# A ConvNeXt-V2 block on one core: the layer-norm chain one slot shorter, and the first expansions two slots later

## The chip, the cores and the metric

The kernel runs on one NeuronCore of a Trainium2 chip. Five engines work side by side, each through its own instruction stream in order: PE (TensorE, matrix products into the eight PSUM banks), ACT (ScalarE), DVE (VectorE), POOL (GpSimd) and SP, which here only issues DMA transfers. The metric is device microseconds (us) from launch to end. Three timed runs of the kernel before took 1468.47, 1468.29 and 1466.35 us; the median is 1468.29 us.

## The reference

One image of 512 x 512 pixels with 96 channels in bfloat16. `K` is 3 and `E` is 384 hidden channels.

```python
for i in range(K):
    for j in range(K):
        out = out + xp[:, i:i+H, j:j+W, :] * dw[i, j][None, None, None, :]
h = _layernorm(out, axis=-1)
h = jnp.einsum('bhwc,ce->bhwe', h, w1)
h = _gelu(h)
gx = jnp.sqrt((h * h).sum(axis=(1, 2), keepdims=True) + 1e-6)
nx = gx / (gx.mean(axis=-1, keepdims=True) + 1e-6)
h = grn_gamma * (h * nx) + grn_beta + h
h = jnp.einsum('bhwe,ec->bhwc', h, w2)
return x + h
```

The sum of `h * h` runs over the whole image, so no output can be made before every pixel has been expanded and passed through the GELU once. The kernel therefore has two phases with a short global step between them.

## The kernel before, in words

The image is cut into 128 blocks of four image rows (`NBLK`, `GR`). Phase 1 is a software pipeline written as a list of numbered slots (the loop at line 852). In slot s the 3x3 convolution of block s runs, for s up to 127, and, once the pipeline is full, the expansion of an older block, called "mlp" in the code: its product with `w1` and the GELU. The distance between the two is the lag. A slot is thus one of three kinds: convolution alone (the ramp), convolution and expansion, or expansion alone (the tail, `NTAIL` slots, `mlp_tail`).

What happens to block b on the way:

- The convolution is three bursts of 24 matmuls (`conv_taps`) into three PSUM banks, `Y3`, banks 4 to 6. In some slots without an expansion, called spare, it takes the banks 0 to 3 that expansions would use. ACT copies the result out (`evac`, tile `y_bf`).
- The squares of `y_bf` are made by ACT in a slot without an expansion (`sqa`), else by POOL one slot later (`sqp`). PE adds up values and squares per pixel (`stage_stats`) into a part of PSUM bank 7.
- Blocks come in batches of 4 (the first three batches, blocks 0 to 3, are smaller and take a shorter path on DVE). When the last block of a batch has its sums, DVE makes the variances (`stage_var`, tile `var`) and clears the sums. POOL makes the first guess of 1/sqrt (`stage_rstd`: 2 small instructions) and two Newton steps (`stage_newton`: 8). DVE transposes the result (`stage_turn`, tile `rt`), SP writes it to DRAM (`stage_rows`, 2 transfers) and reads it back spread over partitions (`stage_bcast`, 4 transfers, tile `rbc`).
- POOL multiplies each block by its `rbc` (`stage_norm`, tile `yn`), SP writes it to DRAM (`stage_write`, 4 transfers) and, one slot later, reads it back in the layout of the expansion (`stage_read`, tile `ynT`).
- The expansion (`mlp_units`) is 9 GELU instructions on ACT of one or two banks each in a slot with a convolution, and 4 of three banks in the tail. DVE takes statistics of the GELU's output (`bst`); part of it is summed through PE instead (`gram_next`, also in bank 7). Every third block up to 111 is kept in DRAM as it is ("whole", 3 stores), the last even blocks stay in SBUF ("held"), and the others are expanded a second time in phase 2.

The slot of every step is set by the loop at line 820, through `put(slot, what, value)`. With `last_s` the slot of the batch's last sums, the old table is: moments at `last_s`, first guess at +1, Newton and turn at +2, rows at +3, bcast at +4, first multiplication at +5. Each later block of a batch follows one slot on; write, read and expansion come 1, 2 and 4 slots after the multiplication. The expansion of a batch whose first block is b0 so begins in slot b0 + 14.

Within one slot the order on each engine is fixed by the loop's text; every instruction keeps program order. SP: load of x for block s + 4, read, write, bcast, rows, one store of a whole block. POOL: Newton, square, multiplication, first guess. DVE in a slot with an expansion: two statistics, the transposes of x for block s + 3 (`turn_x`), two and two more statistics, the transpose of `rt`, the variances, the remaining statistics.

The slots worked out from that table: before, the slots without an expansion are 0 to 4, 7, 10 to 16 and 29, with expansions of blocks 0 to 3 in slots 5, 6, 8 and 9 and of block 4 in slot 17. Slot 29 is one because blocks 12 to 15 were squared by ACT, so their sums came a slot earlier, while block 16's batch took the longer way: block 16 is expanded two slots after block 15. From slot 30 to 127 every slot has both, and 128 to 141 are the tail.

Of the kernel before, what the change touches and what calls it, by code (L numbers as in the profile page):

```python
# [17 lines left out]
BATCH = 4  # L18
NHELD = 5
EVERY = 3  # L20
NTAIL = 14
GRB = 3


# [32 lines left out]
def kernel(  # L57
# [23 lines left out]
    NBLK = H // GR  # L81
# [7 lines left out]

    TAIL0 = NBLK - NTAIL  # L90
    HELD = [NBLK - 2 - 2 * i for i in range(NHELD)][::-1]
# [3 lines left out]
        return q in HELD  # L95

    def is_whole(q):
        return q < TAIL0 and q % EVERY == 0

    def cm_quads(q):  # L100
        if is_whole(q) or is_held(q):
            return NQ
        if q > HELD[0]:
            return 1
        return 2 if q >= NBLK - 16 or q % EVERY == 1 else 3

    whole = [q for q in range(NBLK) if is_whole(q)]
    g_dram = dram.tile([len(whole), 128, NQ * NCH * QW], bf16, name="g_dram")

# [51 lines left out]
    W2s = consts.tile([128, NCH, C], bf16, name="W2s")  # L161
    B2c = consts.tile([128, C], f32, name="B2c")
    free = [[q for q in range(NBLK) if is_whole(q)], list(HELD)]
    free = [v for i, q in enumerate(free[0]) for v in (free[1][i:i + 1] + [q])]
    made_q = KEPT + [q for q in range(NBLK) if not is_whole(q) and not is_held(q) and q not in KEPT]
# [17 lines left out]
    with ExitStack() as p1:  # L183
        pe, dve, act, pool, sp = (InOrder(tc, e) for e in (nc.tensor, nc.vector, nc.scalar, nc.gpsimd, nc.sync))
# [259 lines left out]
        def turn_x(b):  # L444
            xin = xins.pop(b)
            t = xt_ring[b % NXT]
            pairs = t[:, 0:2, :].rearrange("p i s -> p (i s)").bitcast(f32)
            dve.transpose(out=pairs.rearrange("p (g m) -> p g m", m=MB),
                          in_=xin[:, :, 0:64].bitcast(f32))
            dve.transpose(out=t[:, 2, :].rearrange("p (g m) -> p g m", m=MB), in_=xin[:, :, 64:96])  # L450
# [103 lines left out]
        def stage_rstd(k, eng):  # L554
            N = BATCHES[k][1] * GR * NG
            var = msts.pop(k)
            eng.tensor_scalar(out=var[:, :N], in0=var[:, :N], scalar1=3.0e38, scalar2=C * LN_EPS,
                              op0=ALU.min, op1=ALU.max)
            ri = small.tile([128, NS], i32, name="ri")
            eng.tensor_scalar(out=ri[:, :N], in0=var[:, :N].bitcast(i32), scalar1=-0.5, scalar2=float(0x5F3759DF),  # L560
                               op0=ALU.mult, op1=ALU.add)
            rcur = ri[:, :N].bitcast(f32)
            rns[k] = (var, rcur)

        def stage_newton(k, eng):
            N = BATCHES[k][1] * GR * NG
            var, rcur = rns[k]
            for it in range(NEWTON_ITERS):
                last = it == NEWTON_ITERS - 1
                t_ = small.tile([128, NS], f32, name="nt")  # L570
                eng.tensor_tensor(out=t_[:, :N], in0=rcur, in1=rcur, op=ALU.mult)
                eng.tensor_tensor(out=t_[:, :N], in0=t_[:, :N], in1=var[:, :N], op=ALU.mult)
                f = C ** 0.5 if last else 1.0
                eng.tensor_scalar(out=t_[:, :N], in0=t_[:, :N], scalar1=-0.5 * f, scalar2=1.5 * f,
                                  op0=ALU.mult, op1=ALU.add)
                rn = small.tile([128, NS], bf16 if last else f32, name="rstd" if last else "rn")
                if last and N % 32:
                    eng.memset(rn[:, N:(N + 31) // 32 * 32], 0.0)
                eng.tensor_tensor(out=rn[:, :N], in0=t_[:, :N], in1=rcur, op=ALU.mult)
                rcur = rn[:, :N]  # L580
            rns[k] = rn
# [72 lines left out]
        def stage_norm(b, eng=None):  # L654
            k = batch_of[b]
            b0, n = BATCHES[k]
            yn = ynpool.tile([128, NI, W], bf16, name="yn")
            (eng or pool).tensor_tensor(out=yn[:], in0=ybf.pop(b)[:],
                               in1=rbcs[k][:, b - b0:b - b0 + 1, :].to_broadcast([128, NI, W]), op=ALU.mult)
            yns[b] = yn  # L660
# [106 lines left out]
        def store_next():  # L767
            if stores:
                b, h = stores.pop(0)
                n = NCH * QW * NQ // 3  # L770
                sp.dma_start(out=g_dram[whole.index(b)][:, h * n:h * n + n],
                             in_=flat(b)[:, h * n:h * n + n])
# [41 lines left out]
        def put(s, what, v):  # L814
            at.setdefault((s, what), []).append(v)

        RAMP = 4
        last_norm = -1
        mlp_slots = set()
        for k, (b0, n) in enumerate(BATCHES):  # L820
            for b in range(b0, b0 + n):
                quick = b not in mlp_slots
                put(b if quick else b + 1, "sqa" if quick else "sqp", b)
                last_s = b + 1 if quick else b + 2
                put(last_s, "stats", b)
            ramp = b0 + n <= RAMP
            if ramp:
                put(last_s, "chain", k)
                put(last_s + 1, "spread", k)
            else:  # L830
                put(last_s, "moments", k)
                put(last_s + 1, "rstd", k)
                put(last_s + 2, "newton", k)
                put(last_s + 2, "turn", k)
                put(last_s + 3, "rows", k)
                put(last_s + 4, "bcast", k)
            for b in range(b0, b0 + n):
                last_norm = s = max(last_norm + 1, last_s + (1 if ramp else 5))
                put(s, "norma" if ramp else "norm", b)
                put(s + 1, "write", b)  # L840
                put(s + 2, "read", b)
                m = s + (3 if ramp else 4)
                mlp_slots.add(m)
                put(m, "mlp", b)
                put(m + is_whole(b), "combine", b)
                last_slot = m
# [2 lines left out]
        turn_x(0)  # L849
        turn_x(1)  # L850
        turn_x(2)
        for s in range(last_slot + 1):
            get = lambda kind: at.get((s, kind), [])
            if s + 4 < NBLK:
# [8 lines left out]
                stage_rows(k)  # L863
            store_next()
            for k in get("newton"):
                stage_newton(k, pool)
            for b in get("sqp"):
                stage_sq(b, False)
            for b in get("norm"):
                stage_norm(b)  # L870
            for k in get("rstd"):
                stage_rstd(k, pool)
            mlp = get("mlp")

            def spread_out():
# [2 lines left out]
                for b in get("norma"):  # L878
                    stage_norm(b, dve if b < 2 else pool)

            spare = not mlp and s % 2 == 1
            taps, evac = conv_taps(s, spare) if s < NBLK else ([], None)
            if mlp and mlp[0] >= TAIL0:
                assert not taps
# [26 lines left out]
            else:  # L911
                b = mlp[0]
# [165 lines left out]
```

## Time and profile before

| what | value |
|---|---|
| median of three timed runs | 1468.29 us |
| the profiled execution, its time | 1471.49 us |
| the profiled execution, its span | 1469.7 us |
| PE, ACT, DVE, POOL busy in the span | 95%, 95%, 80%, 87% |
| slots 0 to 16, first copy of a convolution to the first GELU of block 4 | 12.19 to 97.28 us |
| slots of both kinds, copy of block 30 to copy of block 127 | 198.06 to 880.25 us, 97 slots of 7.03 us |
| GELU of the tail, one slot | about 5.35 us |
| mean granted TensorE clock | 0.994 |

All durations below come from the one profiled execution. Its time is 3.2 us over the median of the timed runs and 1.8 us over its own span. In the timeline a row gives the start, the time from the first to the last of a merged run of equal instructions, the engine, the operation with its tiles, how many there were, and in brackets how long the engine sat idle before and what released it. In a table of stretches each column gives the busy time of one engine in that stretch, then the granted clock of TensorE (PEclk), the share of the DMA engines' time and the bytes moved.

### The profile page before, as it was taken

The numbers are of one execution on the slowest core, as the hardware profiler recorded it, in microseconds if no ns is written. First come the engines' busy times: TensorE is split into PE (matmuls) and PEld (weight loads), VectorE is DVE, ScalarE is ACT, GpSimd is POOL, SyncE is SP. The second block draws the span as 40 slices with busy tenths as digits, with TensorE's granted clock in tenths as the row PEclk, the third lists the DMA queues.
The fourth block names the chain that finished last, engine by engine and source line by source line (L and its number), as shares of the span: only waits on it lengthen the run. The fifth ranks groups of instructions, "written<-read, shape, count | busy, mean of one in ns | idle before, by whom it ended". The sixth has DMA issues, their size and how long they took to land. (4 is left out here: it accounts for less than half of the span.)

```text
span 1469.7 us, 54337 instructions
## 1 busy us (share of the span) xinstructions
PE 1391.7 (95%) x23105; PEld 816.2 (56%) x23105; DVE 1171.2 (80%) x2232; ACT 1401.4 (95%) x1583; POOL 1278.9 (87%) x864
## 2 busy tenths in 40 slices
PE   7889989999999999999999998789999999999998
PEld 3344444444444444444444455467777777767776
DVE  7749989999999999999999996865555555545555
ACT  6889979999999999999999999999999999989997
POOL 2549899999999999999999896569999999999998
PEclk9999999999999999999999999999999999999999
DMA  5577889889888988888988876659999999999998
GB/s 169 177 216 221 258 259 287 269 261 280 266 261 277 285 249 268 280 271 272 278 265 264 267 244 174 194 194 398 331 356 396 412 396 394 409 387 389 405 399 333
DMA packets 169210, 430.30 MB, mean 293 GB/s; under 512 B 34374, under 2 KB 84230, under 8 KB 164102
## 3 DMA queue, kind: packets, MB, share of 16 engines
q1 hardware_dynamic: 152292, 318.52, 66.5%
q0 software_dynamic: 15312, 108.14, 19.2%
q8 instruction: 181, 2.97, 0.8%
q14 instruction: 63, 0.52, 0.1%
q10 hardware_dynamic: 1362, 0.15, 0.1%
HBM read 265.70 MB, written 160.94 MB: 290 GB/s over the span
## 5 line engine op out<-in xcount | busy, mean ns | idle before, releaser
L35 ACT ACTIVATE g<-PS 128x512 bf16<-128x512 f32 (+2 forms) x1062 | 735.5, 938 | 10.4 <-PE PS L35 9.3
L35 DVE BATCH_NORM_STATS2 bst<-g 128x6 f32<-128x512 bf16 x1107 | 669.9, 673 | 35.7 <-ACT g L35 35.6
L35 ACT ACTIVATE gr<-PS 128x1536 bf16<-128x1536 f32 x348 | 485.9, 1456 | 26.6 <-PE PS L35 21.5
L35 DVE TENSOR_TENSOR o_sb<-PS,xb 128x384 bf16<-128x384 f32 x512 | 275.9, 557 | 223.2 <-PE PS L35 148.7
L35 POOL TENSOR_TENSOR yn<-y_bf,rbc 128x1536 bf16<-128x1536 bf16 x126 | 391.3, 3108 | 55.2 <-DMA rbc<-r_dram 34.6
L324 POOL TENSOR_TENSOR xb<-xr,B2c 128x1536 f32<-128x1536 bf16 x118 | 368.0, 3133 | 1.4
L35 PE MATMUL PS<-xT,Wq 64*32 64x511 bf16 (+1 forms) x9198 | 341.2, 389 | 27.0 <-ACT y_bf L35 11.0
L35 PE MATMUL PS<-ynT,w1p 128*128 128x512 bf16 x1158 | 340.0, 380 | 17.1 <-ACT g L35 5.3
L35 POOL TENSOR_TENSOR ysq<-y_bf 128x1536 bf16<-128x1536 bf16 x114 | 313.2, 2748 | 38.4 <-ACT y_bf L35 35.8
L35 PE MATMUL PS<-ynT,w1s 128*128 128x512 bf16 x984 | 266.8, 380 | 0.0
L35 PEld LDWEIGHTS <-gr 128*128 128x128 bf16 x4152 | 203.7, 98 | 54.7 <-ACT gr L35 0.7
L35 ACT ACTIVATE y_bf<-PS 128x1536 bf16<-128x1536 f32 (+2 forms) x135 | 207.7, 1544 | 16.7 <-PE PS L35 12.6
L35 PEld LDWEIGHTS <-Wq 64*32 64x32 bf16 x9216 | 112.9, 90 | 198.7 <-PE PS L35 112.0
L35 PE MATMUL PS<-W2s,gr 128*128 128x96 bf16 x4080 | 213.1, 206 | 0.3 <-DVE o_sb L35 0.2
L35 DVE STREAM_TRANSPOSE xT<-xin 128x576 f32<-128x576 f32 (+1 forms) x256 | 181.4, 749 | 13.8 <-DMA xin<-in_x_dram 13.7
L35 PEld LDWEIGHTS <-w1p 128*128 128x128 bf16 x1158 | 97.0, 97 | 168.9 <-issue 123.0
L35 PEld LDWEIGHTS <-g 128*128 128x128 bf16 x1716 | 105.8, 98 | 89.1 <-issue 56.0
L35 PE MATMUL PS<-w1p,ynT 128*128 128x256 bf16 (+2 forms) x828 | 125.2, 272 | 7.3 <-ACT xT L35 2.8
L35 PE MATMUL PS<-g 128*128 128x128 bf16 x1476 | 123.8, 220 | 5.9 <-DVE PS L35 5.9
L35 PEld LDWEIGHTS <-gl 128*128 128x128 bf16 x1824 | 90.5, 98 | 41.0 <-issue 20.1
L35 PE MATMUL PS<-W2s,gl 128*128 128x96 bf16 x1824 | 98.1, 207 | 13.1 <-DVE o_sb L35 13.0
L35 PEld LDWEIGHTS <-w1s 128*128 128x128 bf16 x984 | 78.4, 98 | 39.0 <-issue 0.6
(110 smaller groups left out, 672.9 us busy)
## 6 DMA issues: line engine op xcount, KB each, us to landing
g_dram<-g SPq DMA_DIRECT2D x114, 512.0 KB
gl<-g_dram POOLq DMA_DIRECT2D x38, 1536.0 KB, 10.8
xin<-in_x_dram SPq DMA_DIRECT2D x126, 432.0 KB
yn_dram<-yn SPq DMA_DIRECT2D x512, 96.0 KB
ynT<-yn_dram SPq DMA_DIRECT2D x128, 384.0 KB
out_dram<-o_sb SPq DMA_DIRECT2D x127, 384.0 KB
xr<-in_x_dram POOLq DMA_DIRECT2D x123, 384.0 KB, 6.7
ynT<-yn_dram SPq DMA_DIRECT2D x246, 128.0 KB
```

The lines of the kernel that those rows point to most:

```text
L35: r = f(*a, **k)
L324: pq.tensor_tensor(out=xb[:], in0=grp[q]["xr"][:], in1=bias[:, None, :].to_broadcast([128, PXP, C]), op=ALU.add)
```

## The change

Four things, in one edit:

- `stage_rstd` moves from the end of POOL's part of slot `last_s + 1` to right before `stage_newton`, and both now stand at the start of slot `last_s + 1`, ahead of POOL's square and multiplication. Turn, rows, bcast and the first multiplication each move one slot forward. The lag becomes 13, and `NTAIL` 13.
- Blocks 0 to 3 are expanded in slots 7 to 10 instead of 5, 6, 8 and 9.
- A slot without an expansion is spare when it is the second, fourth and so on of a run of such slots, instead of when its number is odd.
- The set of whole blocks keeps its old bound, written as a number.

```diff
-NTAIL = 14
+NTAIL = 13
...
     def is_whole(q):
-        return q < TAIL0 and q % EVERY == 0
+        return q < NBLK - 14 and q % EVERY == 0
...
+        FIRST_MLP = 7
...
-                put(last_s + 1, "rstd", k)
-                put(last_s + 2, "newton", k)
-                put(last_s + 2, "turn", k)
-                put(last_s + 3, "rows", k)
-                put(last_s + 4, "bcast", k)
+                put(last_s + 1, "newton", k)
+                put(last_s + 1, "turn", k)
+                put(last_s + 2, "rows", k)
+                put(last_s + 3, "bcast", k)
             for b in range(b0, b0 + n):
-                last_norm = s = max(last_norm + 1, last_s + (1 if ramp else 5))
+                last_norm = s = max(last_norm + 1, last_s + (1 if ramp else 4))
...
-                m = s + (3 if ramp else 4)
+                m = b + FIRST_MLP if ramp else s + 4
...
+        alone = 0
...
             for k in get("newton"):
+                stage_rstd(k, pool)
                 stage_newton(k, pool)
             for b in get("sqp"):
                 stage_sq(b, False)
             for b in get("norm"):
                 stage_norm(b)
-            for k in get("rstd"):
-                stage_rstd(k, pool)
...
-            spare = not mlp and s % 2 == 1
+            alone = 0 if mlp else alone + 1
+            spare = alone > 0 and alone % 2 == 0
```

Worked out from the new table: the slots without an expansion are 0 to 6 and 11 to 16; the expansions of blocks 0 to 3 stand in slots 7 to 10, that of block 4 still in slot 17, and from there every slot up to 127 has both. Slot 29 now has the expansion of block 16. The tail is slots 128 to 140. Spare are 1, 3, 5, 12, 14 and 16 (before: 1, 3, 7, 11, 13, 15 and 29). Block 114 is expanded beside the last convolution instead of in the tail. The arithmetic and the amount of data moved are the same.

## The prediction, made before the changed kernel ran

> **What bounds the kernel now.** I read the page first, then a table of stretches cut where the slots change kind, then ACT's timeline in the stretches with idle time, then the rows of one batch on POOL and DVE. The page's first part:
>
> ```profile
> PE 1391.7 (95%) x23105; PEld 816.2 (56%) x23105; DVE 1171.2 (80%) x2232; ACT 1401.4 (95%) x1583; POOL 1278.9 (87%) x864
> ```
>
> Two engines at 95% don't say where time can be won. The stretches do (PE, weight loads, DVE, ACT and POOL busy, then clock and DMA):
>
> ```profile
> 180.39:198.06 17.67, 13.26 (x224) 5.88 (x223) 14.19 (x28) 10.27 (x15) 15.48 (x6) 0.81 0.78 231
> 198.06:880.25 682.19, 664.22 (x11933) 331.14 (x11931) 669.33 (x1240) 682.16 (x972) 630.81 (x446) 1.00 0.87 269
> 880.25:961.87 81.62, 65.74 (x635) 42.86 (x633) 64.95 (x128) 78.99 (x62) 50.19 (x28) 1.00 0.61 184
> ```
>
> In the 97 full slots ACT is busy 682.16 of 682.19 us: ACT is the bound, at 682.19 / 97 = 7.03 us a slot. PE stands at 97%, DVE at 98%, POOL at 92%, so all three have little to give. The tail is ACT's too (78.99 of 81.62). Work on ACT is the same after the change but for one square, so the change wins only where ACT is idle. That is ahead of 97 us, in the ramp, and in the first stretch shown: 7.4 us of its 17.67. ACT there, slots 28 to 30:
>
> ```profile
> 180.39 1.51 ACT L35 ACTIVATE y_bf<-PS 128x1536 bf16<-128x1536 f32 x1
> 181.72 2.08 ACT L35 ACTIVATE g<-PS 128x1024 bf16<-128x1024 f32 x3
> 185.81 1.51 ACT L35 ACTIVATE y_bf<-PS 128x1024 bf16<-128x1024 f32 x2 [2.02 <-PE PS L35]
> 187.42 1.48 ACT L35 ACTIVATE ysq<-y_bf 128x1536 bf16<-128x1536 bf16 x1
> 193.36 1.51 ACT L35 ACTIVATE g<-PS 128x1024 bf16<-128x1024 f32 x2 [4.46 <-PE PS L35]
> 195.71 2.49 ACT L35 ACTIVATE g<-PS 128x512 bf16<-128x512 f32 x4 [0.84 <-PE PS L35]
> 198.06 1.49 ACT L35 ACTIVATE y_bf<-PS 128x1536 bf16<-128x1536 f32 x1
> ```
>
> Copies of blocks 28, 29 and 30. Slot 29 has no expansion, and ACT waits for PE three times. PE's rows say why:
>
> ```profile
> 189.50 1.44 PE L35 MATMUL PS<-g 128*128 128x128 bf16 x12 [3.14 <-DVE PS L35]
> 190.87 1.48 PE L35 MATMUL PS<-xT,Wq 64*32 64x512 bf16 x24
> ```
>
> PE stood 3.14 us until DVE had cleared the sums in bank 7, as `gram_next` follows the variances at once in such a slot, and then ran slowly: 24 matmuls of a convolution took 1.48 us, against 0.87 in full slots.
>
> **Part 1: slot 29 becomes a full slot, and one tail slot goes.** Copy 28 to copy 30 is two slots in 17.67 us. After, every slot from 17 to 127 is full. Between copy 28 and copy 127 there are 17.67 + 97 x 7.03 before and 99 x 7.03 after, so 2 x 7.03 - 17.67 = -3.61 us. The tail loses one slot:
>
> ```profile
> 917.01 5.66 ACT L35 ACTIVATE g<-PS 128x1536 bf16<-128x1536 f32 x4
> 922.33 5.71 ACT L35 ACTIVATE xT<-PS 128x1536 bf16<-128x1536 f32 x4
> ```
>
> 922.33 - 917.01 gives 5.3, and 5.35 over the next ones. Sum: -3.61 - 5.35 = **-8.96**. Checked by work: it is the 7.3 us of ACT's idle time, the square of 1.48, and small change. That square goes to POOL, 2.75 us, where 8% are free.
>
> **Part 2: the ramp.** From slot 0 to slot 10 both orders hold 11 convolutions, 7 squares on ACT and 4 expansions. Before, ACT ends them at 74.06, after waits of 2.71 (for the first `ynT`), 1.00, 0.19, 3.31 (slot 7: spare convolution waits for the expansions' banks) and 1.08 us from slot 5 on, 8.3 in all. After, slots 5 and 6 are two more convolutions, during which the first `ynT` lands, and slots 7 to 10 are full ones without a change of banks. I leave 1.1 us of wait for slot 5 (slot 4 had 1.11) and 0.6 for slot 7 (the convolution's first burst waited 0.64 to 0.90 for its banks): slot 10 ends at 74.06 - 8.3 + 1.7 = 67.5. The next six slots, 11 to 16, end when block 4 can be expanded. That hangs on a chain. Variances of blocks 4 to 7: end of slot 9, at 67.5 - 7.0 - 0.4 = 60.1. `rt` on DVE 6.55 later (below): 66.7. From `rt` to the first multiplication took 72.48 to 83.44, POOL waiting 12.49 us for `rbc` before it: 10.96, so 77.6. Newton steps for blocks 8 to 11 now stand ahead of it on POOL: their variances came 1.4 after copy 12 (78.52 to 79.9), copy 12 is due at 72.3 by steps of 3.4 to 4.0 a slot, and 3.6 us of Newton end at 77.3, hidden behind `rbc`. From that multiplication to the first GELU of block 4 took 97.28 - 83.44 = 13.84: 91.4, against 97.28, so -5.9. Bounds: convolution alone (3.43 a slot, copies at 71.10 and 74.53) would give 88.7, so -8.6; a chain that is no earlier gives 0.
>
> In that chain PE waits some 2 us for `ynT` in slot 17. Rows: after 3.14 us idle it ran slowly, as shown, and after an idle 1.88 us at 46.7 a convolution of 72 took 4.13 us, against 2.81. So I add 1.5 us, 0.62 for three matmuls of the first unit (1.44 against 0.82) and 0.84 for the wait at 195.71: **-4.4**. [...]
>
> **Part 3: the chain in every batch, 28 times in full slots.** One batch before, on DVE and on POOL:
>
> ```profile
> 419.15 0.22 DVE L35 TENSOR_TENSOR var<-PS,neg 128x64 f32<-128x64 f32 x1
> ...
> 432.95 0.23 DVE L35 STREAM_TRANSPOSE rt<-rstd 128x64 bf16<-128x64 bf16 x1
> ```
>
> ```profile
> 423.61 0.24 POOL L35 TENSOR_SCALAR var<-var 128x64 f32<-128x64 f32 x1
> ...
> 448.56 3.11 POOL L35 TENSOR_TENSOR yn<-y_bf,rbc 128x1536 bf16<-128x1536 bf16 x1
> ...
> 674.58 3.11 POOL L35 TENSOR_TENSOR yn<-y_bf,rbc 128x1536 bf16<-128x1536 bf16 x1 [0.78 <-DMA rbc<-r_dram]
> ```
>
> The 10 small POOL instructions take 3.55 us (423.61 to 427.14) wherever they stand. New wait one: POOL's first guess waits for `var`, and square and multiplication queue behind it. Without waits POOL needs 3.55 + 4 x 5.78 (a square and a multiplication, 427.14 to 432.91) = 26.7 us a batch, the batch has 4 x 7.03 = 28.1, so it may idle 1.4. It now does so here instead of at squares (22.4 us of such waits from 200 to 870). Cost nothing. New wait two: `rt` waits for POOL, and DVE's statistics queue behind. `rt` stood 13.58 after the end of `var` (419.37); one slot less leaves 6.55, and 3.65 are needed: 2.9 us to spare. Cost nothing as long as POOL is less than that late. SP: two `rows` (1.19 us) and four `bcast` (2.55) move one slot forward, past a load of x, a read, four writes and a store; their order among themselves stays. The write after the first multiplication starts later, at `var` + 9.4 instead of + 7.5 (426.84), and holds SP that long; the expansion it feeds comes three slots on. The loop that can bind: POOL's first guess, multiplication, write, the read that waits for its landing, next write, `bcast`, `rbc`, multiplication, next first guess. It is the same before and after. Where POOL did not wait for `rbc`, its first guess to that multiplication took 24.95 (423.61 to 448.56), a ceiling; where it waited, up to 25.7 (648.9 to 674.58). With 3.2 to the next guess that is 28.1 to 28.9 against 28.13, but only 3 waits, 1.9 us in all, name `rbc` from 200 to 870. So the mean is under 28.1. Taken: 0; bounds: -0 (ACT is full) and + 28 x 0.8 - 2.9 = +19.5.
>
> **Sum.** -8.96 - 4.4 = -13.4. On the profiled execution's 1471.49 that is 1458.1; the median stood 3.2 lower, so I forecast **1455.0 us** for timed runs.
>
> **Rivals.** A: as above, 1455, chance 0.58. B: the ramp gives nothing back, since the chain to block 4 starts at the end of slot 9 now and not of slot 8, and convolutions merely wait in another place: -9.0, 1459.3. For it: POOL waited 12.49 us for `rbc` in the ramp, so DMA sets the pace there. Against: 8.3 us of ACT waits ahead of it have no cause left. Chance 0.17. C: slot 29's gap returns as a late block 16. Its `rbc` was late before (the multiplication at 169.64 had waited 6.08 us) and its expansion now has one slot of convolution less ahead. All but 4 us come back: 1464. Chance 0.10. D, slower: the loop of part 3 binds. POOL then falls behind every batch, and once 2.9 us are used up `rt` holds DVE, whose 98% can't make it up. It decides from 0.58 us a batch on ((13.4 + 2.9) / 28); with 1.1 us a batch, 1455 + 30.8 - 2.9 = 1483. For it: 25.7 us above, and a turn that did wait 3.59 us for POOL at 90.24. Against: the few waits on `rbc`. Chance 0.15, of which 0.11 end slower, 0.02 the same and 0.02 faster.
>
> **Range and chances.** A's own is 1449 to 1458 (the best ramp -8.6 and no slow clock give 1450.7). B and C lie above; 1449 to 1467 leaves out D's slower part and little more. I take 0.2% (2.9 us) as what a measurement tells from no change. Faster: 0.58 + 0.17 + 0.07 of C + 0.02 = 0.84; same 0.05; slower 0.11.
>
> **What would show it.** Right: no full-slot stretch without an expansion near 185 us; ACT's first GELU of block 4 near 91; copy 17 to copy 127 at 7.03 a slot; 13 tail slots; POOL's waits on `var` instead of on `y_bf`. Wrong: `rt` waiting for POOL in many batches, a slot over 7.05, waits for `ynT` on PE after 100 us, or a first GELU of block 4 at 97.

## The result, and the profile after

The changed kernel takes 1457.95 us (median of five timed runs, 1455.90 to 1460.28), the kernel before, timed beside it, 1468.29 us (1466.35 to 1471.13). The ratio is 0.9923 with a 95% interval of 0.9908 to 0.9938: the medians lie 10.3 us apart, and the interval is worth 9.1 to 13.5 us. The forecast was 1455.0, so its sign and its order of size were right, and it promised 3 us too much.

The profiled execution of the changed kernel took 1455.9 us, with a span of 1454.0 us. Its page starts:

```profile
PE 1387.2 (95%) x23105; PEld 815.3 (56%) x23105; DVE 1170.2 (80%) x2232; ACT 1398.7 (96%) x1586; POOL 1280.3 (88%) x865
```

As before, the shares of the whole span hide the change. The table of stretches shows it (start and end, length, then PE, weight loads, DVE, ACT and POOL busy, granted clock, DMA share, GB/s). The cuts are the starts of ACT's copies of blocks 0, 10, 17, 28, 30 and 127:

```profile
12.57:63.95 51.38, 44.85 (x986) 20.23 (x987) 40.99 (x103) 47.16 (x56) 15.28 (x17) 1.00 0.60 186
63.95:95.66 31.71, 27.88 (x729) 13.15 (x727) 18.38 (x38) 25.09 (x27) 23.25 (x27) 1.00 0.63 192
95.66:172.88 77.22, 74.25 (x1328) 36.58 (x1326) 75.07 (x137) 77.22 (x111) 68.89 (x42) 1.00 0.85 262
172.88:186.95 14.07, 13.74 (x250) 6.87 (x248) 13.82 (x28) 14.07 (x22) 12.25 (x15) 1.00 0.91 290
186.95:869.18 682.23, 665.50 (x11939) 331.65 (x11937) 670.82 (x1244) 682.23 (x971) 629.92 (x436) 1.00 0.86 269
```

For the kernel before, the first three of these stretches were not shown yet:

```profile
12.19:71.10 58.91, 49.17 (x1024) 21.71 (x1009) 44.84 (x109) 48.09 (x58) 20.89 (x18) 0.94 0.56 175
71.10:101.01 29.91, 26.41 (x712) 12.06 (x709) 14.79 (x32) 24.45 (x23) 15.14 (x14) 1.00 0.63 184
101.01:180.39 79.38, 74.07 (x1328) 36.12 (x1326) 73.44 (x134) 78.11 (x112) 64.52 (x50) 1.00 0.81 246
```

From copy 17 to copy 127, ACT is now busy in every microsecond of the profiled execution: 77.22 of 77.22, 14.07 of 14.07, 682.23 of 682.23. Before it was busy 78.11 of 79.38 in the same eleven slots, and 10.27 of 17.67 around slot 29. The 97 full slots did not move. The granted clock of the first stretch rose from 0.94 to 1.00, which the forecast had not looked at.

ACT's timeline of the changed kernel, slots 28 to 30, shows two full slots of 7.03 us with no wait in brackets, where the row of 4.46 us stood:

```profile
172.88 1.66 ACT L35 ACTIVATE y_bf<-PS 128x1536 bf16<-128x1536 f32 x1
174.21 6.02 ACT L35 ACTIVATE g<-PS 128x1024 bf16<-128x1024 f32 x9
179.91 1.67 ACT L35 ACTIVATE y_bf<-PS 128x1536 bf16<-128x1536 f32 x1
181.24 6.03 ACT L35 ACTIVATE g<-PS 128x1024 bf16<-128x1024 f32 x9
186.95 1.66 ACT L35 ACTIVATE y_bf<-PS 128x1536 bf16<-128x1536 f32 x1
```

And POOL's groups in the full slots (window 187 to 869; after the bar the busy time, the mean, and the idle time just ahead with what ended it) show where its waits went:

```profile
L35 POOL TENSOR_TENSOR yn<-y_bf,rbc 128x1536 bf16<-128x1536 bf16 x97 | 301.2, 3106 | 27.2 <-DMA rbc<-r_dram 18.5 <-DMA g_dram<-g 5.9 <-DMA xin<-in_x_dram 2.4
L35 POOL TENSOR_TENSOR ysq<-y_bf 128x1536 bf16<-128x1536 bf16 x98 | 269.0, 2745 | 0.1
L35 POOL TENSOR_SCALAR var<-var 128x64 f32<-128x64 f32 x24 | 5.7, 239 | 7.2 <-DVE var L35 5.8
```

The squares waited 22.4 us for `y_bf` before and wait for nothing now. But most of that idle time did not go to `var`, as the forecast had it: the multiplications now wait 27.2 us, 18.5 of them with `rbc`, the end of the loop, as the releaser. The timeline puts practically all of these 27.2 us ahead of the first multiplication of a batch, the one that needs the new `rbc`.

The stages, from the starts of ACT's copies, in two executions of each kernel (us; the last column is what the forecast's steps gave):

| stretch | before | before, second | after | after, second | forecast of the difference |
|---|---|---|---|---|---|
| copy 0 to copy 10 | 58.91 | 58.45 | 51.38 | 51.40 | |
| copy 10 to copy 17 | 29.91 | 29.76 | 31.70 | 32.90 | together -4.4 |
| copy 17 to copy 28 | 79.38 | 79.41 | 77.22 | 77.51 | 0 |
| copy 28 to copy 30 | 17.67 | 15.90 | 14.07 | 14.07 | -3.61 |
| copy 30 to copy 127 | 682.19 | 682.22 | 682.23 | 682.23 | 0 |
| copy 127 to the scaling of `w2` | 86.74 | 87.89 | 81.79 | 83.00 | -5.35 |
| the rest to the end | 502.72 | 503.54 | 503.06 | 503.65 | 0 |

### The profile page after: what moved, and what is told of

Same layout as the page of the kernel before. It is cut to its first block, busy times and chain, and to the rows that moved or that the text cites. A ratio compares the mean times of both kernels' runs of the same rounds, so it can differ in the third digit from the quotient of the medians.

```text
span 1454.0 us, 54342 instructions
## 1 busy us (share of the span) xinstructions
PE 1387.2 (95%) x23105; PEld 815.3 (56%) x23105; DVE 1170.2 (80%) x2232; ACT 1398.7 (96%) x1586; POOL 1280.3 (88%) x865
## 4 chain that ended last, share of the span: by engine, by line
PE 29%; ACT 25%; DVE 16%; POOL 13%; DMA 8%; issue 5%; SPq 3%; POOLq 0%; ACTq 0%; DVEq 0%
PE PS L35 29%; ACT g L35 17%; DVE bst L35 10%; POOL xb L324 9%; ACT y_bf L35 7%; SPq L35 3%; DMA xin<-in_x_dram 3%; DVE xT L35 3%; DMA ynT<-yn_dram 2%; DMA rbc<-r_dram 2%; DMA yn_dram<-yn 2%; POOL yn L35 2%; ACT xT L35 1%; DVE o_sb L35 1%; POOL nt L35 1%
## 5 line engine op out<-in xcount | busy, mean ns | idle before, releaser
L35 ACT ACTIVATE gr<-PS 128x1536 bf16<-128x1536 f32 x348 | 485.9, 1456 | 26.7 <-PE PS L35 21.7
L35 ACT ACTIVATE y_bf<-PS 128x1536 bf16<-128x1536 f32 (+1 forms) x134 | 209.7, 1569 | 12.4 <-PE PS L35 12.3
```

Source lines behind the costliest of these rows:

```text
L35: r = f(*a, **k)
```

## The experiments

The results below give medians of timed runs, and ratios to the kernel before, timed on the same chip; a gain in us is that ratio times the median of the kernel before, unless two times are compared. Stage times are from the one profiled execution of each kernel.

**The kernel before, once more, and the changed one.** No edit; these are the second columns of the table above.

> The kernel before once more, unchanged, for a second profile. Theory S (the small waits of slots 17 to 28 belong to the kernel): the copies of blocks 17 to 28 again lie some 79.4 us apart, 2.2 us over eleven full slots, and the copies of blocks 28 and 30 some 17.7 us apart. Theory R (those waits are chance of one execution): 17 to 28 takes 77.4 us, and the span is nearer to 1466.

One execution, 1471.26 us. Copy 17 to copy 28 took 79.41 again, so the 2 us by which these eleven full slots exceed 11 x 7.03 belong to the kernel. Copy 28 to copy 30 took 15.90 instead of 17.67: the size of slot 29's stall is not fixed. PE's row for it, in this second execution:

```profile
188.28 1.37 PE L35 MATMUL PS<-g 128*128 128x128 bf16 x12 [2.32 <-DVE PS L35]
```

It waited 2.32 us for DVE where the forecast's execution had 3.14, and the granted clock from copy 28 to copy 30 was 0.89 instead of 0.81.

> The changed kernel unchanged, once more beside the kernel before on this chip, for a second profile and a firmer ratio. Expected: -9 to -14 us, copies 17 to 127 at 7.03 us a slot again, first GELU of block 4 near 92 us.

1458.12 us, ratio 0.9919 [0.9906, 0.9932], so 11.9 us faster here. The stages repeat within 0.3 us, but for copy 10 to 17 and the tail (1.2 us each) and the rest (0.6). The first GELU of block 4 came at 92.86.

**The ramp alone, with the lag of 14.** The kernel before with the first expansions in slots 7 to 10 and the new rule for spare banks:

```diff
-                m = s + (3 if ramp else 4)
+                m = b + 7 if ramp else s + 4
...
+        alone = 0
...
-            spare = not mlp and s % 2 == 1
+            alone = 0 if mlp else alone + 1
+            spare = alone > 0 and alone % 2 == 0
```

> The kernel before with the first expansions in slots 7 to 10 and the new rule for spare banks alone; chain, lag of 14 and tail of 14 slots stay. No slot without an expansion is left after slot 17. My theory: -7 to -11 us against before, most of the gain, with the first GELU of block 4 near 95 us, the copies of blocks 18 to 127 at 7.03 us a slot, and no turn waiting for POOL. Rival (the shorter chain is what pays): 0 to -4 us.

1458.47 us, ratio 0.9925 [0.9912, 0.9938]: 11.0 us faster, as much as the whole change within the intervals, and the first GELU of block 4 at 94.09. In this order block 4 is expanded in slot 18 and slot 29 is full: the one slot without an expansion has moved from 29 to 17. There it takes 3.55 us (copy 16 to copy 17), where around slot 29 copy 28 to copy 30 was 1.8 to 3.6 us longer than two full slots. Copy 17 to copy 28 is 77.71, copy 28 to 30 is 14.06, and the tail, still of 14 slots, is 88.36.

**The shorter lag alone, with the old ramp.** The changed kernel with the old ramp slots and the old rule for spare banks:

```diff
-                m = b + FIRST_MLP if ramp else s + 4
+                m = s + (3 if ramp else 4)
...
-            spare = alone > 0 and alone % 2 == 0
+            spare = not mlp and s % 2 == 1
```

> The changed kernel with the old ramp: first expansions in slots 5, 6, 8 and 9 and spare banks in odd slots; only the shorter chain and the tail of 13 slots stay. A slot without an expansion is left alone in the full stretch again, now slot 28. My theory (the gain is the lone slot and the ramp's waits): 0 to -4 us against before, since one tail slot of 5.35 and one ramp slot of 3.5 become one full slot of 7.03. Rival (the shorter chain is what pays): -8 to -12 us, nearly all of the change.

In this kernel the sums of block 28 are added in before the variances of the batch of blocks 24 to 27 are taken, so block 28's sums are mixed into block 24's; the amount of work is the same. 1463.97 us, ratio 0.9963 [0.9949, 0.9976]: 5.4 us faster, more than the theory's 4 and less than the rival's 8. The slot without an expansion in the full stretch is now 28, and it takes no variances. Copy 17 to copy 30 came to 75.63 + 13.58 = 89.2 us, where twelve full slots and one of 3.43 would be 87.8; before it was 97.05 and 95.31. So the stall is gone here as well, and the tail is shorter (81.95). But copy 0 to copy 17 grew from 88.2 or 88.8 to 92.2 (57.54 + 25.54 + 9.15), and that took some 3.5 us back. In this order block 4 is expanded in slot 16, so copy 15 to copy 16 took 6.65 us instead of 3.40, and copy 16 to copy 17 took 9.15 instead of 6.69, with PE waiting 0.78 us for `ynT` and 1.66 us for the cleared sums.

The two halves give 11.0 + 5.4 us alone and 11 to 12 together. Once the ramp is in the new order, the shorter lag is worth nothing that can be measured here. Against the ramp-only kernel, the changed one saves 5.4 to 6.6 us in the tail (88.36 to 83.00 or 81.79) and pays 4.5 to 5.7 us up to copy 17 (78.60 to 83.09 or 84.30), because slot 17 now holds an expansion: 7.0 us instead of 3.5, and PE's waits ahead of it. An expansion moved out of the tail is not saved. It is moved into a slot with a convolution, at 7.03 - 3.43 = 3.6 us, so at best 5.35 - 3.6 = 1.75 us are won. In the profiled executions these were lost up to copy 17: the step from copy 16 to copy 17 took 7.76 and 6.65 us with PE waiting for the first `ynT`, and copy 10 to copy 16 took 23.95 and 26.25 against the ramp-only kernel's 23.66.

**What Newton's place costs.** The changed kernel with the guess and Newton steps behind POOL's square and multiplication of the slot:

```diff
-            for k in get("newton"):
-                stage_rstd(k, pool)
-                stage_newton(k, pool)
             for b in get("sqp"):
                 stage_sq(b, False)
             for b in get("norm"):
                 stage_norm(b)
+            for k in get("newton"):
+                stage_rstd(k, pool)
+                stage_newton(k, pool)
```

> The changed kernel with POOL's ten small instructions behind its square and multiplication of the same slot instead of ahead of them; everything else stays. Newton then ends some 8.8 us after the variances instead of 3.65, and the turn on DVE, which stands 7.1 us after them, waits. Theory D (as in the forecast's slower rival: what DVE loses it loses in every batch, at 98% busy): 1.6 us for each of 28 batches, +45 us against the changed kernel. Theory L (a loss that settles: square and multiplication hang on ACT's copy and not on the variances, so once DVE is a little later Newton is in time again): 0 to +4 us, with many short waits of the turn.

1459.61 us (1457.57 to 1464.27), ratio 0.9932 [0.9906, 0.9959], so within about 2 us of the changed kernel, as theory L has it and not theory D. In the profiled execution, which was the slowest of these, copy 30 to 127 took 686.80, 4.6 us more, and copy 28 to 30 took 16.03. `rt` still ran 7.1 to 7.9 us behind `var` with short waits for POOL, so the two orders settle almost alike.

**A longer and a shorter loop.** The changed kernel with three Newton steps in place of two, and with one (`NEWTON_ITERS = 1`; the second step is left out there, so the root is coarser):

```diff
-NEWTON_ITERS = 2
+NEWTON_ITERS = 3
```

> The changed kernel with a third Newton step: four more small POOL instructions, 1.25 us, in every batch, in the loop first guess, multiplication, write, read, write, bcast, multiplication, first guess. Theory T (the loop stands right at the 28.13 us of a batch, so every addition to it shows): the loop takes 28.0 + 1.25 us, POOL falls behind about 1 us a batch, and after two batches the turn holds DVE: +20 to +32 us against the changed kernel. Theory W (the waits for bcast are slack that a later POOL takes up): 0 to +4 us.

> The changed kernel with one Newton step instead of two, in every batch (the second step is left out, so the root is coarser). The counterpart of the run with three steps. Theory T (the loop of one batch stands just under the batch's period, ACT sets it): 1.25 us less in a loop that doesn't bind gives nothing, copy 30 to copy 127 stays 682.2 and the time is within 2 us of the changed kernel's; POOL's lateness behind var shrinks. Rival U (the loop already costs something in the changed kernel, spread over ramp and tail): 3 us or more are gained.

Three steps: 1495.86 us, ratio 1.0161 [1.0125, 1.0198], 35 to 38 us slower than the changed kernel (by the ratios and by the medians), which is more than theory T's 32. In the profiled execution, the slowest of four, 26.3 us of it lie in the 97 full slots (708.51); most of the rest is in the ramp (90.08 to copy 17) and the tail (89.86). One step: 1457.37 us, ratio 0.9919 [0.9903, 0.9936], the same as two, with 682.23 in the full slots. POOL's and DVE's groups say why. With three steps (window 187 to 900; the second block is the answer for the tile `rt`, with the idle time of DVE ahead of it and its number of waits):

```profile
L35 POOL TENSOR_TENSOR yn<-y_bf,rbc 128x1536 bf16<-128x1536 bf16 x97 | 301.5, 3108 | 27.4 <-DMA rbc<-r_dram 11.0 <-DMA g_dram<-g 10.3 <-DMA xin<-in_x_dram 4.5
L35 POOL TENSOR_SCALAR var<-var 128x64 f32<-128x64 f32 x25 | 6.0, 239 | 2.1
```

```profile
L35 DVE STREAM_TRANSPOSE rt<-rstd x24: 226/245/249, 198.5 to 871.8; 128x64 bf16<-128x64 bf16 x24
its engine sat idle before it (us, times) until:
  POOL rstd L35: 15.9, 16
```

With one step (window 187 to 869):

```profile
L35 POOL TENSOR_TENSOR yn<-y_bf,rbc 128x1536 bf16<-128x1536 bf16 x98 | 304.7, 3109 | 12.5 <-DMA rbc<-r_dram 8.6 <-DMA g_dram<-g 3.5 <-POOL ysq L35 0.2
L35 POOL TENSOR_SCALAR var<-var 128x64 f32<-128x64 f32 x24 | 5.8, 241 | 51.6 <-DVE var L35 51.5
```

The idle time ahead of `var` is POOL's reserve. With one step POOL waits 51.5 us for DVE there, about 2 us in every batch; with two, 5.8 us in all (11.1 in the second execution); with three, nothing names `var` (2.1 us are the gaps between instructions), POOL comes late to every batch, and `rt` holds DVE 16 times. One Newton step is four POOL instructions, some 1.5 us with their gaps. Taking it away wins nothing, adding it costs 26 us in the full slots: the changed kernel stands just inside the edge. POOL's own work would not explain that: by the forecast's 26.7 us a batch it is 28.2 with the third step, under 0.1 more than a batch has, at most 2 us in 24 batches. The rest is the 27.4 us of waits ahead of the multiplications, again the first of a batch.

**Slot 29's stall by itself.** The kernel before, with the Gram products left for the next slot when a slot without an expansion takes variances:

```diff
-                gram_next(2)
+                if not get("moments"):
+                    gram_next(2)
```

> The kernel before, where slots without an expansion that hold variances leave their two Gram products to the next slot. Only slot 29 has any at that place. My theory (2.3 to 3.1 us of the 10 us that slot 29 costs are PE waiting for the cleared sums, and 0.5 to 1.5 us the slow clock after it): -2 to -4.5 us against before. Rival (block 16 comes late anyhow, so another wait takes its place): 0 to -1 us.

1467.36 us, ratio 0.9982 [0.9969, 0.9995]: 2.6 us faster. Copy 28 to copy 30 fell to 12.26, and PE's row in that place now reads

```profile
186.52 0.89 PE L35 MATMUL PS<-xT,Wq 64*32 64x512 bf16 x24
```

with neither the wait for DVE nor the slow matmuls (before: 1.48 us for the same 24). So the wait for the cleared sums did set that slot. Part of what it gave was lost again, with copy 17 to copy 28 at 80.53; the granted clock is 0.98 there (101 to 180), where the kernel before has 1.00 in both executions, and whether the edit brings that on is not shown.

**The rule for spare banks.** The changed kernel with `spare = not mlp and s % 2 == 1`:

> The changed kernel with the old rule for spare banks (odd slots): spare are 1, 3, 5, 11, 13 and 15 instead of 1, 3, 5, 12, 14 and 16. Slot 11 then takes the banks that the expansion of slot 10 has just filled. My theory (a change of banks right after an expansion costs the 1 to 2 us that slot 7 cost before, but the chain to block 4 hides most of it): 0 to +2 us against the changed kernel, with PE waiting 1 us or more for g at the start of slot 11. Rival (the rule for spare banks carries the gain of the ramp): +4 to +7 us.

1458.80 us, ratio 0.9923 [0.9904, 0.9941]: no difference that can be told from the changed kernel's time. PE did wait 1.07 us for `g` at the start of slot 11, and copy 0 to copy 17 took 85.89 us in the profiled execution, 1.6 to 2.8 us more than in the changed kernel, but the timed runs don't show it. This part of the change is worth nothing measurable.

**Later first expansions, looking for a better version.** The changed kernel with the first expansions in slots 9 to 12, and in slots 13 to 16 (`FIRST_MLP = 13`), where no slot after the first expansion is without one; block 4 is held in slot 17 in both:

```diff
-        FIRST_MLP = 7
+        FIRST_MLP = 9
...
-                last_norm = s = max(last_norm + 1, last_s + (1 if ramp else 4))
+                last_norm = s = max(last_norm + 1, last_s + 1 if ramp else max(last_s + 4, b + 9))
```

> The changed kernel with the first expansions in slots 9 to 12 instead of 7 to 10, block 4 still in slot 17. Theory R (what is left in the ramp is ACT's and PE's wait ahead of block 4): the sums of block 7 now come after slots of convolution alone, about 10 us earlier, so slot 17 finds its ynT and the step from copy 16 to copy 17 is 7.0 us (6.65 to 7.75 before). By the slots' own lengths in the changed kernel (3.73 us for each of the first five, 3.99 for slots 10 to 15): copy 0 to copy 17 in 8 x 3.73 + 5.1 + 4 x 7.0 + 3 x 4.0 + 7.0 = 81.9 us against 83.1 to 84.3, time 1 to 2 us below the changed kernel. Rival (slots of convolution alone are set by the loads and transposes of x, which get less far ahead in a longer run of them): copy 0 to copy 17 at 83 to 86, time 0 to 3 us above.

> The changed kernel with blocks 0 to 3 expanded in slots 13 to 16, so that no slot without an expansion comes after the first with one. Theory R: 12 x 3.73 + 5.1 + 4 x 7.0 = 77.9 us from copy 0 to copy 17, 5 us below the changed kernel's 83.1, and no wait of PE for ynT in slot 17; the time is 4 to 6 us lower. Rival (x sets the pace of a long run of convolutions, 4.6 us every second slot): 83 us or more, time the same or up to 3 us longer.

Slots 9 to 12: 1460.74 us, ratio 0.9943 [0.9928, 0.9957]; slots 13 to 16: 1458.53 us, ratio 0.9927 [0.9912, 0.9942]. Neither beats the changed kernel. The step from copy 16 to copy 17 fell to 6.65 and 7.03 us as the theory said, but copy 0 to copy 17 took 86.7 and 83.5, against 83.1 to 84.3. So the rival was right about the length (86.7 is even beyond its 86), though not about its cause: in the second kernel slots 6 to 8 of the long run took 3.42 to 3.45 us each. In the first kernel the stall of slot 29 comes back in slot 13, where the variances of the batch of blocks 8 to 11 are now taken (PE's timeline):

```profile
78.55 1.13 PE L35 MATMUL PS<-g 128*128 128x128 bf16 x12 [2.70 <-DVE PS L35]
79.61 3.95 PE L35 MATMUL PS<-xT,Wq 64*32 64x512 bf16 x72
```

In the second, PE ran slowly for two slots behind a wait of 1.15 us (its granted clock is 0.91 from 12.4 to 71.1):

```profile
48.84 0.44 PE L35 MATMUL PS<-rowsel,y_bf 128*128 128x4 bf16 x12 [1.15 <-ACT y_bf L35]
...
49.51 3.68 PE L35 MATMUL PS<-xT,Wq 64*32 64x512 bf16 x72
...
53.85 4.33 PE L35 MATMUL PS<-xT,Wq 64*32 64x512 bf16 x72
```

## Why the prediction was right, and where it was off

**The bound.** Right. ACT sets 97 slots at 7.03 us in both kernels, and the change won nothing there. From copy 17 to copy 127 ACT now has no idle time in the first execution and 0.2 us in the second.

**Part 1, slot 29 and the tail slot.** The mechanism of slot 29 was right: leaving out the wait for the cleared sums alone shortened it. -3.61 for slot 29 is exact for the execution that it was read from (17.67 to 14.07), but the second execution of the kernel before had 15.90, so the term is 1.8 to 3.6 us. The tail gave 3.7 to 6.1 us by the pairs of executions, around the forecast's 5.35. What the step did not see is that the two terms do not need the shorter lag: the ramp-only kernel removes slot 29's stall too, and the tail's slot is paid for in slot 17. So the times of these stretches came out about right, while the shorter lag, which both terms were reasoned from, was not needed for the gain.

**Part 2, the ramp.** -4.4 forecast; copy 0 to copy 17 gave 3.9 to 5.7 us. Its chain came out nearly to the instant: slot 10's last GELU, forecast to end at 67.5, ended at 67.51, `rt` of the first batch forecast at 66.7 ran at 66.9, and the first GELU of block 4, forecast at 91.4 without and 92.9 with a charge for a slow clock, started here:

```profile
91.93 3.90 ACT L35 ACTIVATE g<-PS 128x1024 bf16<-128x1024 f32 x6 [1.00 <-PE PS L35]
```

The wait that carried the charge is there as forecast, 1.97 us for `ynT` in slot 17, but the matmuls after it were not slow (three in 0.82 us, against 1.44 in the kernel before at 32.00):

```profile
91.29 0.82 PE L35 MATMUL PS<-ynT,w1p 128*128 128x512 bf16 x3 [1.97 <-DMA ynT<-yn_dram]
92.04 0.89 PE L35 MATMUL PS<-xT,Wq 64*32 64x512 bf16 x24
```

So the charge of 1.5 us failed as put: the granted clock stayed at 1.00 from 66.90 to 95.66. In the second execution a slow stretch came elsewhere, behind a shorter idle time (the granted clock is 0.94 from 70 to 97):

```profile
80.31 1.35 PE L35 MATMUL PS<-xT,Wq 64*32 64x511 bf16 x29 [1.45 <-issue]
...
82.28 4.12 PE L35 MATMUL PS<-xT,Wq 64*32 64x512 bf16 x72
```

Behind an idle time of 1.45 us a convolution of 72 matmuls took 4.12 us instead of 2.81. A charge of about this size (1.31 us here) is right for some executions and not for others; what decides it was not shown. The new ramp also has lost two such stretches of the old one, which stand at these waits (PE's timeline of the kernel before, whose granted clock is 0.50 from 31.67 to 35.08 and from 48.74 to 52.15):

```profile
32.00 1.44 PE L35 MATMUL PS<-ynT,w1p 128*128 128x512 bf16 x3 [2.26 <-DMA ynT<-yn_dram]
...
48.61 4.13 PE L35 MATMUL PS<-xT,Wq 64*32 64x512 bf16 x72 [1.88 <-ACT g L35]
```

The forecast counted the second of them only inside ACT's waits. With them gone the clock of the first stretch went from 0.94 to 1.00. It is 0.94 there in the ramp of both executions of the kernel before, of the shorter lag alone and of the later Gram products, and 1.00 with the first expansions in slots 7 to 10, but for the kernel with three Newton steps (0.97, cut at 66.0).

**A term that was missing.** Copy 17 to copy 28 was costed at nothing and gave 1.9 to 2.2 us. Before, these slots ran up to 7.8 us (8.4 in the second execution), and ACT had 1.27 and 1.56 us of waits in them; in the profile it was there to be read, as 79.38 is more than 11 x 7.03 = 77.3. The ramp-only kernel has 77.71, so the new order of the ramp removes it. Which wait of the old ramp is behind it was not isolated.

**Part 3, the chain in every batch.** Cost nothing: right, since the full slots took 682.23. The reason given was too comfortable. The turn had 2.9 us to spare by the forecast, and in the changed kernel POOL's first guess came up to 2.94 us behind `var` (the batch of blocks 44 to 47) before it caught up; in the second execution up to 2.19, and none of it was left by block 48. One batch, DVE and then POOL, with POOL some 1.75 us late and `rt` on time:

```profile
408.70 0.23 DVE L35 TENSOR_TENSOR var<-PS,neg 128x64 f32<-128x64 f32 x1
...
415.84 0.23 DVE L35 STREAM_TRANSPOSE rt<-rstd 128x64 bf16<-128x64 bf16 x1
```

```profile
410.68 0.24 POOL L35 TENSOR_SCALAR var<-var 128x64 f32<-128x64 f32 x1
...
413.94 0.32 POOL L35 TENSOR_TENSOR rstd<-nt,rn 128x64 bf16<-128x64 f32 x1
...
434.87 3.12 POOL L35 TENSOR_TENSOR yn<-y_bf,rbc 128x1536 bf16<-128x1536 bf16 x1 [0.61 <-DMA rbc<-r_dram]
```

From the guess to that multiplication took 24.19 us; with a wait on `rbc` at its end, the loop is closed and sets POOL's pace. SP's issues in between fit it: a write at 420.35, when the multiplication had ended at 420.04, the read at 426.23, the next write at 426.60 and `bcast` at 429.23. The next guess came at 438.07, 27.39 us after the first, so POOL gains 0.7 us on the 28.13 of a batch. Rival D's mechanism therefore exists, and the run with three Newton steps shows it at full price; by an estimate it lacks some 0.4 us a batch to bind, as 1.5 us more in the loop cost 1.1 (26.3 us in 24 batches).

**The rivals.** B (the ramp gives nothing) is ruled out by the stages, not by the time: 1459.3 lies among the times measured (1455.90 to 1460.28), but copy 0 to copy 17 shrank by 3.9 us at least. Part of its mechanism is there: of the 7.1 to 7.5 us won up to copy 10, 1.8 to 3.1 were lost again by copy 17. C (slot 29's stall comes back as a late block 16) is ruled out by 14.07 us for copy 28 to copy 30. D did not bind.

**The sum.** The step that was off is the last one: -13.4, worked out within one execution, was taken off a median that stood 3.2 us below that execution. On the profiled frame 1458.1 was forecast, and the two profiled executions took 1455.9 and 1458.8. But the medians differ by 10.3 and 12.2 us. A likely reason is that the stalls that the change removes (slot 29's, the slow stretches of PE) are themselves part of what makes one execution longer than another: slot 29 alone was 1.8 us apart in two executions, and of the 13 timed runs of the kernel before that stood beside the changed one's second runs, the five with a mean granted clock of 0.995 took 1467.0 to 1469.6 us, the eight with 0.991 to 0.994 took 1469.3 to 1472.0. An execution that is 3 us above the median then holds more of them, and the difference to the median should have been taken off the gain, wholly or in part. How much of the 3 us this is was not measured.

## What to carry to other kernels

When a software pipeline is cut by one slot, count what the expansion taken out of the tail costs in the slot that it moves into; here 5.35 us became at most 1.75, and the slots without an expansion mattered more by their place than by their number: in the ramp one cost 3.55 us, in the middle, at slot 29, it stalled PE on a bank that DVE was clearing (3.14 and 2.32 us), and at slot 28, where no variances fall, it did not. A loop through several engines and DRAM that ACT hides is not safe because it costs nothing today: adding one unit of work to it and taking one away, as with three Newton steps and one, shows how far the edge is. And a gain summed from the stalls of one execution belongs to that execution; take it off its own time, not off a faster median.

## What the hardware showed that was not expected

TensorE's slow stretches did not follow the length of the idle time ahead. Behind 1.88 us idle (the kernel before), 1.45 us (the changed kernel, second execution) and 2.70 us (first expansions in slots 9 to 12), 72 matmuls took 4.13, 4.12 and 3.95 us, against 2.81; behind 1.97 us in the changed kernel three took 0.82 us, against 1.44 when slow. The slow stretch behind the 1.88 us cost its convolution 1.3 us (4.13 - 2.81); the one behind 1.15 us, with the first expansions in slots 13 to 16, cost two convolutions 2.4 us (3.68 and 4.33, against 2.81 each).

The granted clock shows where the slow stretches lie. Leaving out the last 2 us of each trace, it is 0.50 in the kernel before from 31.67 to 35.08, 48.74 to 52.15, 188.68 to 195.51 and 1318.49 to 1321.90, and in the changed kernel from 1301.94 to 1305.35 alone. Around the 1.88 us and the 1.97 us it reads as follows; the first two rows are the kernel before, the others the changed one:

```profile
45.32:48.74 3.42, 1.54 (x32) 0.83 (x24) 3.42 (x7) 3.42 (x6) 2.20 (x2) 1.00 0.90 276
48.74:52.15 3.41, 3.24 (x64) 0.76 (x61) 2.81 (x5) 0.80 (x2) 1.73 (x1) 0.50 0.88 264
86.80:90.21 3.41, 2.42 (x78) 1.20 (x72) 1.32 (x2) 2.91 (x4) 3.39 (x2) 1.00 0.71 236
90.21:93.63 3.42, 2.34 (x31) 0.89 (x32) 1.54 (x8) 2.42 (x4) 2.49 (x9) 1.00 0.76 221
```

The 1.88 us ended at 48.61, and the clock was 0.50 from 48.74 on. The 1.97 us ended at 91.29, and the clock stayed at 1.00. What makes the difference is not shown. Slot 29's stall went with 6.83 us of half clock in the first execution of the kernel before and, by an estimate from its granted clock, with (1 - 0.89) x 15.90 / 0.5 = 3.5 us in the second; at half speed the difference is worth 1.7 us, about that between 17.67 and 15.90.

That transfers could hold up GpSimd without costing a microsecond was also new here: 18.5 us of waits on `rbc` in the changed kernel, and 8.6 with one Newton step, go with the same 682.23 us.
